# Running half of w1's sums for both chunks early, and pairing the second chunk's attention, in a fused attention and max-out feed-forward kernel

## The chip, the cores and the metric

The kernel runs on one core of a Trainium2 chip. The metric is device time in microseconds (us), lower is better.

The trace records when TensorE's clock is granted at full and when at half rate. The half-rate records are 3.4 us long or a multiple of it, but for the one that the end of the profile can cut: in e12 it begins at 406.85 of 408.3 us, with the work all but done, and makes a mean clock of 0.998. A run's mean clock shows how many others it had: 0.998 to 1.0 for none, about 0.996 for one, 0.992 or less for two or more.

## The reference

```python
def attn(q, k, v, E, F):            # batch 8, heads 8, seq 1024, head_dim 64
    k_proj = einsum('ks,bhsd->bhkd', E, k)       # 64 projected keys
    v_proj = einsum('ks,bhsd->bhkd', F, v)
    scores = q @ k_proj.T / 8
    p = exp(scores - max); p /= p.sum()
    return p @ v_proj
def moe(x, w1, w2, w3, w_out):      # x: 8192 x 512, w1..w3: 512 x 768
    return maximum(maximum(x @ w1, x @ w2), x @ w3) @ w_out
```

The output of the attention, heads side by side, is x. All matrix work is in bf16.

## The kernel before

A batch has four pairs of heads (pair = "g") and two chunks of 512 positions. The four pairs are also the four contraction blocks ("ct") of x @ w, so w's sums over ct 0 and 1 need only pairs 0 and 1. For batch 0, whose inputs are still being loaded, the kernel starts w1 on these two while pairs 2 and 3 are not yet there.

In the traces each engine runs its instructions in the order in which the program gives them. The program has a small clock model of its own; it serves only to choose one of the eight PSUM banks (PSUM is the memory into which TensorE writes) for each result. Several names matter:

- `scores` and `exps`: score matmuls of a pair, and exp of them (pT).
- `z` (sums, then Ln and Exp(-) on ScalarE: zi = 1/sum) and `x` (values, then a VectorE multiplication by zi into xT).
- `k_pair`: projects a pair's keys; VectorE copies them to kpT. `v_pair` does it for values. `kproj(1)`: the keys of batch 1.
- `qp`, `q_duo`: transpose q. `idle(n)`: n filler matmuls on a tile of zeros.

```python
    def up_first(work):                       # batch 0, chunk 0
        ...
        h = six()                             # six banks
        for ct in range(2):
            for jt in jts:
                up_mm(h[jt][0], 0, 0, 0, jt, (ct,), last=1)          # w1
                if ct == 1:
                    copy("sv"[jt % 2], s1[:, jt], *h[jt])            # evict
        then(0)          # q_duo(1), k_pair(2), k_pair(3), scores and exps of
                         # pairs 2 and 3, idle(2), z(2), z(3)
        load_k1()
        h = six()
        for ct in range(2):
            for jt in jts:
                up_mm(h[jt][0], 1, 0, 0, jt, (ct,))                  # w2
            then(1 + ct)                      # 1: v_pair(2); 2: x(2), v_pair(3)
        for jt in jts:
            up_mm(h[jt][0], 1, 0, 0, jt, (2,))
            if jt == 2:
                then(3)                       # x(3)
        ...                                   # w1 ct 2, 3; w2 ct 3; then w3
    def up(b, ch, jt):                        # every other chunk: a step per jt
        ...                                   # w1, w2, w3: four matmuls each
        h1s = ffn_sb.tile([P, CHUNK], FP32, name="h1s")
        nc.scalar.copy(out=h1s, in_=h[0][0])
        ...
        nc.vector.tensor_tensor(out=m12, in0=h[1][0], in1=h1s, op=ALU.max)
        most(hTs[b, ch][:, jt, :], *h[2], m12)                       # VectorE max
    ...
    # plan of batch 0 (chunk, step): second-chunk attention behind w3 and down,
    # then batch 1's attention behind chunk 1's steps
        (0, 6): [za(0, 1, *c1), sc(0, 3, *c1), ld(1)],
        (0, 7): [za(0, 2, *c1)],
        (0, 8): [za(0, 3, *c1)],
        (0, 9): [kproj(1)],
        (1, 0): [kt(1), qp(1, (0,)), qp(1, (1,))],
        ...
        (1, 3): [za(1, 0), sc(1, 3)],
        (1, 4): [za(1, 1)],
        (1, 5): [za(1, 2)],
```

The softmax here doesn't subtract the row's maximum and nothing guards it: scores larger than these inputs give would overflow.

## Time and profile before

| | before |
|---|---|
| time, median | 408.5 us (408.05 to 408.85) |
| span of the profiled run, its mean clock | 407.8 us, 0.996 |
| start of kproj(1) (ends chunk 0 of batch 0) | 48.78 us |
| from there to batch 1's first w1 matmul ("chunk 1's stage") | 29.80 us |

The first part of the page gives busy time per engine, as share of the span. PE is TensorE's matmuls, DVE is VectorE, ACT is ScalarE, POOL is GpSimd.

```profile
span 407.8 us, 6116 instructions
PE 393.8 (97%) x2452; PEld 180.4 (44%) x2497; DVE 202.3 (50%) x311; ACT 192.9 (47%) x281; POOL 34.9 (9%) x46
```

TensorE is nearly always busy, so the gain has to come from its few idle stretches. The table of stretches of the same run shows where they are; a row gives the stretch, its length, and busy time (with the number of instructions) of PE, PEld, DVE, ACT and POOL, then the mean clock, the share of the DMA engines as the view gives it (it can exceed 1) and their GB/s.

```profile
16.50:31.00 14.50, 12.27 (x142) 6.15 (x142) 5.82 (x12) 5.07 (x9) 3.31 (x4) 1.00 1.21 206
...
48.78:78.58 29.80, 29.14 (x239) 13.64 (x243) 17.21 (x26) 17.45 (x23) 2.62 (x3) 1.00 0.83 153
```

Only 2.2 us are idle in the first row. The list of waits for TensorE in 16 to 49 us names what ended each wait; these are the four longest:

```profile
PE banks L288 <- DVE xT L257: 0.8, 1, 0.8
PE banks L207 <- DVE kpT L99: 0.5, 1, 0.5
PE banks L227 <- DVE vp L99: 0.4, 1, 0.4
PE banks L227 <- ACT pT L218: 0.2, 1, 0.2
```

The first is v_pair(3), which waits until x(2)'s multiplication has left the bank; the second is the scores of pair 2, which wait for the kpT copy. No load is in the list.

### The profile page before, as it was taken

The page shows a single profiled execution, that of the slowest core. Times are in us where ns is not written, and L with a number is a line of the kernel's source. Part 1 is how long each engine was busy: PE and PEld are TensorE (multiplying, and loading weights), DVE is VectorE, ACT ScalarE, POOL GpSimd, SP SyncE. Part 2 cuts the span into 40 slices and gives each one's busy share as a digit, 9 for nine tenths or more (in the row PEclk, how much of TensorE's full clock was granted, in tenths as well). Part 3 has the DMA queues.
Part 4 walks back from the last instruction along what each step waited for, and adds up shares of the span by engine and source line. Part 5 has one row for each costly group of instructions (what it writes and reads, how often), then busy time and mean ns, then how long its engine had stood idle before and what let it go on. Part 6 is the DMA issues. An engine that isn't in the chain of part 4 may idle for free.

```text
span 407.8 us, 6116 instructions
## 1 busy us (share of the span) xinstructions
PE 393.8 (97%) x2452; PEld 180.4 (44%) x2497; DVE 202.3 (50%) x311; ACT 192.9 (47%) x281; POOL 34.9 (9%) x46
## 2 busy tenths in 40 slices
PE   7879999999999999999999999999999999999995
PEld 2534454344444544444544445444544444444443
DVE  1429665473465527636453565525464363525251
ACT  2432537623764266547445555537535555432322
POOL 7325002002000200200010002000000000000000
PEclk9899999999999999999999999999999999999999
DMA  9999939959926994893799109960520202020202
GB/s 152 206 207 206 220 98 145 251 122 127 244 42 161 191 247 123 121 242 54 182 184 204 52 13 243 203 161 0 123 87 0 104 2 103 2 103 0 104 0 104
DMA packets 58492, 52.30 MB, mean 128 GB/s; under 512 B 25952, under 2 KB 54112, under 8 KB 58464
## 3 DMA queue, kind: packets, MB, share of 16 engines
q0 software_dynamic: 28496, 28.31, 43.8%
q1 hardware_dynamic: 29824, 23.46, 17.9%
q8 instruction: 19, 0.31, 0.3%
q10 hardware_dynamic: 144, 0.13, 0.1%
q14 instruction: 9, 0.07, 0.1%
HBM read 57.15 MB, written 16.78 MB: 181 GB/s over the span
## 4 chain that ended last, share of the span: by engine, by line
PE 91%; DMA 3%; ACT 2%; DVE 2%; issue 1%; POOL 0%; ACTq 0%; DVEq 0%; POOLq 0%
PE banks L460 60%; PE banks L586 19%; PE banks L227 4%; PE banks L288 4%; DMA k_t<-in_k_dram 2%; PE banks L207 2%; PE banks L299 1%; ACT zl L240 1%; DVE xT L257 1%; ACT pT L218 1%; DMA out_dram<-o_sb 0%; DVE s L99 0%; ACT zi L246 0%; DVE m L551 0%; ACT o_sb L99 0%
## 5 line engine op out<-in xcount | busy, mean ns | idle before, releaser
L460 PE MATMUL banks<-xT,w_sb 128*128 128x512 bf16 x1118 | 255.1, 379 | 2.1 <-issue 0.5
L460 PEld LDWEIGHTS <-w_sb 128*128 128x128 bf16 x1152 | 109.4, 98 | 137.0 <-issue 10.7
L551 DVE TENSOR_TENSOR m<-banks,h1s 128x512 f32<-128x512 f32 x90 | 62.0, 689 | 86.1 <-ACT h1s L547 54.7
L547 ACT COPY h1s<-banks 128x512 f32<-128x512 f32 x90 | 52.5, 583 | 92.5 <-PE banks L460 89.2
L586 PE MATMUL banks<-wout_sb,hT 128*128 128x512 bf16 x369 | 84.8, 379 | 0.7 <-DVE hT L470 0.2
L257 DVE TENSOR_TENSOR xT<-banks,zi 128x1024 bf16<-128x1024 f32 (+1 forms) x36 | 39.8, 1106 | 78.4 <-ACT zi L246 53.7
L470 DVE TENSOR_TENSOR hT<-banks,m 128x512 bf16<-128x512 f32 x90 | 62.3, 692 | 10.1 <-PE banks L227 0.5
L99 ACT COPY o_sb<-banks 128x512 f32<-128x512 f32 (+1 forms) x60 | 34.9, 581 | 53.0 <-PE banks L586 53.0
L586 PEld LDWEIGHTS <-hT 128*128 128x128 bf16 x378 | 36.0, 98 | 45.5 <-issue 3.1
L240 ACT ACTIVATE zl<-banks 128x1024 f32<-128x1024 f32 (+1 forms) x36 | 33.5, 931 | 30.8 <-PE banks L227 30.6
L218 ACT ACTIVATE pT<-banks 128x1024 bf16<-128x1024 f32 (+1 forms) x36 | 33.2, 931 | 9.7 <-PE banks L207 9.7
L246 ACT ACTIVATE zi<-zl 128x1024 f32<-128x1024 f32 (+1 forms) x36 | 34.6, 962 | 1.1
L196 POOL DMA_DIRECT2D q_t<-in_q_dram x7 | 6.2, 883 | 194.1 <-DMA qT<-q_p 72.1
L288 PEld LDWEIGHTS <-efT 128*64 128x64 bf16 x288 | 14.5, 116 | 4.5 <-issue 4.1
L227 PE MATMUL banks<-pT,ones 64*64 64x512 bf16 (+1 forms) x144 | 14.0, 379 | 1.5 <-ACT pT L218 0.9
L207 PE MATMUL banks<-qT,kpT 64*64 64x512 bf16 (+1 forms) x144 | 13.1, 360 | 0.9 <-DVE kpT L99 0.5
L227 PE MATMUL banks<-pT,vp 64*64 64x512 bf16 (+1 forms) x144 | 13.4, 359 | 0.4 <-DVE vp L99 0.4
L99 DVE CAST vp<-banks 64x256 bf16<-64x256 f32 (+1 forms) x18 | 7.1, 397 | 10.7 <-PE banks L288 7.1
L288 PE MATMUL banks<-v_t,efT 128*64 128x256 bf16 (+1 forms) x176 | 10.7, 271 | 0.9 <-DVE xT L257 0.8
L227 PEld LDWEIGHTS <-ones 64*64 64x64 bf16 x144 | 4.5, 103 | 15.4 <-issue 15.3
L99 ACT CAST vp<-banks 64x256 bf16<-64x256 f32 x14 | 5.1, 365 | 7.3 <-PE banks L288 7.1
L99 DVE COPY q_p<-q_t 128x1024 bf16<-128x1024 bf16 x24 | 8.5, 419 | 0.0
(47 smaller groups left out, 106.7 us busy)
## 6 DMA issues: line engine op xcount, KB each, us to landing
out_dram<-o_sb SPq DMA_DIRECT2D x30, 512.0 KB, 3.1
k_t<-in_k_dram POOLq DMA_DIRECT2D x7, 1024.0 KB, 14.0
q_t<-in_q_dram POOLq DMA_DIRECT2D x7, 1024.0 KB, 9.6
v_t<-in_v_dram POOLq DMA_DIRECT2D x7, 1024.0 KB, 18.5
w_sb<-in_moe_w_dram POOLq DMA_DIRECT2D x6, 384.0 KB, 14.8
k_t<-in_k_dram POOLq DMA_DIRECT2D x2, 512.0 KB, 11.0
v_t<-in_v_dram POOLq DMA_DIRECT2D x4, 256.0 KB, 11.5
wout_sb<-in_moe_w_out_dram POOLq DMA_DIRECT2D x1, 768.0 KB, 16.3
```

What stands on the lines that cost most here:

```text
L99: done = {"v": nc.vector.tensor_copy, "s": nc.scalar.copy, "g": nc.gpsimd.tensor_copy}[eng](out=o, in_=i)
L218: nc.scalar.activation(out=pTs[b, g, lo], in_=t, func=AF.Exp, scale=scale)
L227: nc.tensor.matmul(out=t[hp * HALF:(hp + 1) * HALF, c, 0:nsi * HALF], lhsT=w(rows, hp), rhs=p[rows, hp, :], start=True, stop=True,)
L240: nc.scalar.activation(out=zl, in_=t, func=AF.Ln)
L246: nc.scalar.activation(out=zi, in_=zl, func=AF.Exp, scale=-1.0)
L257: nc.vector.tensor_tensor(out=xTs[b][:, g, lo:lo + nsi, :].rearrange("a (c s) p -> a c (s p)", c=2), in0=t, in1=zi, op=ALU.mult,)
L288: nc.tensor.matmul(out=t[hh * HALF:(hh + 1) * HALF, 0:width], lhsT=efT[:, si, kv - 1, :], rhs=qkv[b][kv][:, heads[hh], si, :], start=(si = ...
L460: nc.tensor.matmul(out=h, lhsT=w_sb[i][:, ct, jt * P:(jt + 1) * P], rhs=xTs[b][:, ct, ch * SPC:(ch + 1) * SPC, :], start=(ct == first), st ...
L470: nc.vector.tensor_tensor(out=o, in0=h, in1=other, op=ALU.max)
L547: nc.scalar.copy(out=h1s, in_=h[0][0])
L551: nc.vector.tensor_tensor(out=m12, in0=h[1][0], in1=h1s, op=ALU.max)
L586: nc.tensor.matmul(out=o_ps, lhsT=hTs[b, ch][:, jt, tt * P:(tt + 1) * P], rhs=wout_sb[:, jt, :], start=(jt == 0), stop=(jt == NJT - 1),)
```

## The change

The intent: give TensorE more to do while pairs 2 and 3 are made ready. With the second chunk's attention of pairs 0 and 1 done early, w1's first half can be made for both chunks ahead. The half sums of chunk 1 wait in SBUF (s1[1]) and are added in when chunk 1 comes. The attention of the second chunk is done for two pairs at once, with 128x1024 instead of 128x512 tiles on ScalarE.

```diff
     load_w(0, 0)
+    load_q(LO, slice(SPC, SI))
     load_q(HI, slice(0, SPC))
 ...
+    def za2(b, gs, lo):                       # two pairs: sums, Ln, Exp, values,
+        def f():                              # two multiplications
 ...
+    def add_s1(ch, jt, t, ns):
+        if jt % 2 == 0:
+            nc.vector.tensor_tensor(out=s1[ch][:, jt], in0=t, in1=s1[ch][:, jt], op=ALU.add)
+            return runs("v", clock["pe"], 0.69, ns)
+        h1s = ffn_sb.tile([P, CHUNK], FP32, name="h1s")
+        copy("s", h1s, t, ns)
+        nc.gpsimd.tensor_tensor(out=s1[ch][:, jt], in0=s1[ch][:, jt], in1=h1s, op=ALU.add)
 ...
+        for jt in jts:
+            up_mm(h[jt][0], 0, 0, 0, jt, (0,), last=1)
+        qp(0, (0, 1), *C1)()
+        for jt in jts:
+            up_mm(h[jt][0], 0, 0, 0, jt, (1,), last=1)
+            if jt == 2:
+                sc2(0, (0, 1), SPC, now=True)()
+            copy("sv"[jt in (1, 2, 4, 5)], s1[0][:, jt], *h[jt])
+        q_duo(1)
+        za2(0, (0, 1), SPC)()
+        k_pair(2)
+        k_pair(3)
+        for g in (2, 3):
+            exps(0, g, *C0, scores(0, g, *C0))
         load_k1()
+        for jt in jts:
+            t, ns = bank()
+            up_mm(t, 0, 0, 1, jt, (0, 1), last=1)          # chunk 1
+            if jt in (0, 1):
+                z(2 + jt)
+            copy("sv"[jt in (1, 2, 4, 5)], s1[1][:, jt], t, ns)
+            if jt == 3:
+                v_pair(2)
 ...                                           # x(2), v_pair(3), x(3) among w2's matmuls
     def up(b, ch, jt):
+        split = (b, ch) == (0, 1)
+            if split and i == 0:
+                up_mm(h[i][0], i, b, ch, jt, range(2, NCT - early), first=2)
 ...
+        if split:
+            h1s = s1[1][:, jt]
+            r = add_s1(1, jt, *h[0])
 ...
-                (0, 6): [za(0, 1, *c1), sc(0, 3, *c1), ld(1)],
-                (0, 7): [za(0, 2, *c1)],
-                (0, 8): [za(0, 3, *c1)],
+                (0, 6): [za2(0, (2, 3), SPC), ld(1)],
```

More of the change, by code (lines that the diff above doesn't have):

```diff
@@ L178 @@
     load_w(2, 1)
-    load_q(ALL, slice(SPC, SI))
+    load_q(HI, slice(SPC, SI))
     nc.gpsimd.dma_start(out=wout_sb, in_=moe_w_out.rearrange("(jt p) m -> p jt m", p=P))
@@ L281, in f, with sc2, exps2 @@
             scale_x(b, g, lo, nsi, av)
+        return f
+    N2 = SPC * HALF
+    def sc2(b, gs, lo, now=False):
+        def f():
+            t, ns = two()
+            for i, g in enumerate(gs):
+                for c in range(2):
+                    for hp in range(2):
+                        rows = slice(hp * HALF, (hp + 1) * HALF)
+                        at = g * SI + lo + c * SPC // 2
+                        nc.tensor.matmul(
+                            out=t[c * HALF:(c + 1) * HALF, hp, i * N2:(i + 1) * N2],
+                            lhsT=kpTs[b][rows, g, :],
+                            rhs=qTs[b][rows, at:at + SPC // 2, :],
+                            start=True, stop=True,
+                        )
+            ready = pe(0.4)
+            def exps2():
+                p = att.tile([P, 2, CHUNK], BF16, name="pT", bufs=4)
+                pTs[b, gs, lo] = p
+                nc.scalar.activation(out=p, in_=t, func=AF.Exp, scale=scale)
+                runs("s", ready, 1.0, ns)
+            if now:
+                exps2()
+            else:
+                later.append(exps2)
+        return f
@@ new lines, in za2, with f @@
+    def za2(b, gs, lo):
+        def f():
+            p = pTs[b, gs, lo]
+            z, zns = two()
+            for c in range(2):
+                rows = slice(c * HALF, (c + 1) * HALF)
+                for hp in range(2):
+                    nc.tensor.matmul(
+                        out=z[hp * HALF:(hp + 1) * HALF, c],
+                        lhsT=ones[rows], rhs=p[rows, hp, :], start=True, stop=True,
+                    )
+            ready = pe(0.23)
+            zl = att.tile([P, 2, CHUNK], FP32, name="zl", bufs=1)
+            nc.scalar.activation(out=zl, in_=z, func=AF.Ln)
+            runs("s", ready, 1.0, zns)
+            zi = att.tile([P, 2, CHUNK], FP32, name="zi", bufs=2)
+            nc.scalar.activation(out=zi, in_=zl, func=AF.Exp, scale=-1.0)
+            when = runs("s", ready, 1.0)
+            t, ns = two()
+            for i, g in enumerate(gs):
+                for c in range(2):
+                    rows = slice(c * HALF, (c + 1) * HALF)
+                    for hp in range(2):
+                        nc.tensor.matmul(
+                            out=t[hp * HALF:(hp + 1) * HALF, c, i * N2:(i + 1) * N2],
+                            lhsT=vps[b][rows, 2 * g + hp, :],
+                            rhs=p[rows, hp, i * N2:(i + 1) * N2],
+                            start=True, stop=True,
+                        )
+            pe(0.3)
+            for i, g in enumerate(gs):
+                cols = slice(i * N2, (i + 1) * N2)
+                nc.vector.tensor_tensor(
+                    out=xTs[b][:, g, lo:lo + SPC, :].rearrange("a (c s) p -> a c (s p)", c=2),
+                    in0=t[:, :, cols], in1=zi[:, :, cols], op=ALU.mult,
+                )
+                runs("v", when, 0.69, ns)
@@ L429, in q_duo @@
         )
-    C0 = (0, SPC)
+    C0, C1 = (0, SPC), (SPC, SPC)
     idle(11)
@@ L471, in most, with up_first @@
         return runs("v", max(clock["pe"], ready), 0.69, ns)
-    def up_first(work):
-        def then(key):
-            run_later()
-            for f in work.get(key, []):
-                f()
-        s1 = ffn_sb.tile([P, NJT, CHUNK], FP32, name="s1", bufs=1)
-        s2 = ffn_sb.tile([P, NJT, CHUNK], FP32, name="s2", bufs=1)
+    s1 = [ffn_sb.tile([P, NJT, CHUNK], FP32, name=f"s1_{ch}", bufs=1) for ch in range(2)]
+    def add_s1(ch, jt, t, ns):
[5 more added lines that the diff above has]
+        nc.gpsimd.tensor_tensor(out=s1[ch][:, jt], in0=s1[ch][:, jt], in1=h1s, op=ALU.add)
+        return clock["s"] + 1.3
+    def up_first():
         hTs[0, 0] = ffn_sb.tile([P, NJT, CHUNK], BF16, name="hT")
@@ L489, in up_first @@
         h = six()
-        for ct in range(2):
-            for jt in jts:
-                up_mm(h[jt][0], 0, 0, 0, jt, (ct,), last=1)
-                if ct == 1:
-                    copy("sv"[jt % 2], s1[:, jt], *h[jt])
-        then(0)
-        load_k1()
-        h = six()
-        for ct in range(2):
-            for jt in jts:
-                up_mm(h[jt][0], 1, 0, 0, jt, (ct,))
-            then(1 + ct)
+        for jt in jts:
[12 more added lines that the diff above has]
+            exps(0, g, *C0, scores(0, g, *C0))
+        load_k1()
+        for jt in jts:
[6 more added lines that the diff above has]
+                v_pair(2)
+        h = six()
+        for jt in jts:
+            up_mm(h[jt][0], 1, 0, 0, jt, (0,))
+            if jt == 1:
+                x(2)
+            if jt == 3:
+                v_pair(3)
+        for jt in jts:
+            up_mm(h[jt][0], 1, 0, 0, jt, (1,))
+            if jt == 1:
+                x(3)
         for jt in jts:
             up_mm(h[jt][0], 1, 0, 0, jt, (2,))
-            if jt == 2:
-                then(3)
+        joined = [0.0] * NJT
         for jt in jts:
@@ L508, in up_first @@
             up_mm(t, 0, 0, 0, jt, (2, 3), first=2)
-            if jt % 2:
-                copy("s", s2[:, jt], t, ns)
-                nc.gpsimd.tensor_tensor(
-                    out=s1[:, jt], in0=s1[:, jt], in1=s2[:, jt], op=ALU.add
-                )
-                added = clock["s"] + 1.3
-            else:
-                nc.vector.tensor_tensor(out=s1[:, jt], in0=t, in1=s1[:, jt], op=ALU.add)
-                added = runs("v", clock["pe"], 0.69, ns)
-            up_mm(h[jt][0], 1, 0, 0, jt, (3,))
-            if jt % 2 == 0:
-                most(s1[:, jt], *h[jt], s1[:, jt], added)
-            elif jt > 2:
-                most(s1[:, jt - 2], *h[jt - 2], s1[:, jt - 2], last)
-            if jt % 2:
-                last = added
-        most(s1[:, 5], *h[5], s1[:, 5], last)
-        then(4)
+            joined[jt] = add_s1(0, jt, t, ns)
+            up_mm(h[jt][0], 1, 0, 0, jt, (3,))
+            for j in ((jt,) if jt % 2 == 0 else (jt - 2,) if jt > 2 else ()):
+                most(s1[0][:, j], *h[j], s1[0][:, j], joined[j])
+        most(s1[0][:, 5], *h[5], s1[0][:, 5], joined[5])
         for jt in jts:
@@ L529, in up_first @@
             up_mm(t, 2, 0, 0, jt, range(NCT))
-            most(hTs[0, 0][:, jt, :], t, ns, s1[:, jt])
-            then(5 + jt)
+            most(hTs[0, 0][:, jt, :], t, ns, s1[0][:, jt])
+            if jt == 2:
+                qp(0, (2, 3), *C1)()
+            if jt == 4:
+                sc2(0, (2, 3), SPC, now=True)()
     def up(b, ch, jt):
@@ L537, in up @@
         early = jt == 0
+        split = (b, ch) == (0, 1)
         for i in range(3):
             h.append(bank())
-            up_mm(h[i][0], i, b, ch, jt, range(NCT - early))
+            if split and i == 0:
+                up_mm(h[i][0], i, b, ch, jt, range(2, NCT - early), first=2)
+            else:
+                up_mm(h[i][0], i, b, ch, jt, range(NCT - early))
             done.append(clock["pe"])
@@ L545, in up @@
                 done[i] = clock["pe"]
-        h1s = ffn_sb.tile([P, CHUNK], FP32, name="h1s")
-        nc.scalar.copy(out=h1s, in_=h[0][0])
-        r = runs("s", done[0], 0.6, h[0][1])
+        if split:
+            h1s = s1[1][:, jt]
+            r = add_s1(1, jt, *h[0])
+        else:
+            h1s = ffn_sb.tile([P, CHUNK], FP32, name="h1s")
+            nc.scalar.copy(out=h1s, in_=h[0][0])
+            r = runs("s", done[0], 0.6, h[0][1])
         run_later()
@@ L609, in plan @@
         if b == 0:
-            c1 = (SPC, SPC)
             return {
-                (0, 6): [za(0, 1, *c1), sc(0, 3, *c1), ld(1)],
-                (0, 7): [za(0, 2, *c1)],
-                (0, 8): [za(0, 3, *c1)],
+                (0, 6): [za2(0, (2, 3), SPC), ld(1)],
                 (0, 9): [kproj(1)],
@@ L672 @@
             if (b, ch) == (0, 0):
-                c1 = (SPC, SPC)
-                def attend():
-                    q_duo(1)
-                    k_pair(2)
-                    k_pair(3)
-                    for g in (2, 3):
-                        exps(0, g, *C0, scores(0, g, *C0))
-                    idle(2)
-                    for g in (2, 3):
-                        z(g)
-                up_first({
-                    0: [attend],
-                    1: [lambda: v_pair(2)],
-                    2: [lambda: x(2), lambda: v_pair(3)],
-                    3: [lambda: x(3)],
-                    5: [qp(0, (0, 1), *c1)],
-                    6: [qp(0, (2, 3), *c1)],
-                    7: [sc(0, 0, *c1)],
-                    8: [sc(0, 1, *c1)],
-                    10: [za(0, 0, *c1), sc(0, 2, *c1)],
-                })
-                run_later()
+                up_first()
                 behind(0, NJT - 1)
```

## The prediction

> **What bounds it now.** TensorE: 97% busy over a span of 407.8 us (page, part 1), 91% of the chain that ended last. From 50 us on it is over 98% busy at full clock, and the change removes no matmul there. Only the first 50 us can give something. The table of stretches shows 12.27 us of TensorE busy in 16.5-31 us: 2.2 us idle, plus 0.4 us of filler matmuls (idle(2)). The waits there: kpT (0.5), pT (0.2), twice the bank that scale_x holds (0.8 and 0.3), and small ones. These 2.6 us (0.6%) are all that the change can win. Loads are not the limit: in 16-50 us no TensorE wait names a DMA. By the load queue's bytes, k's high half lands about 18.7 us; 0.25 MB more ahead of it adds 1.3 us, still in time.
>
> **What changes, by durations of the trace.**
> - Removed: idle(2), 0.4 us. Exp/Ln/Exp of 128x512 tiles (0.60 us) are paired to 128x1024 (1.03).
> - Moved: 12 w1 matmuls of chunk 1 (12 x 0.216 = 2.6 us) ahead of w2, as filler for pairs 2 and 3; the second chunk's attention of pairs 0, 1 (about 1.9 us of TensorE) to around the second w1 quarter.
> - Added: six evictions of half sums (0.6 us each); in chunk 1 three VectorE adds (0.69) and three GpSimd adds (1.31).
>
> **Critical path.** The moved matmuls stand *after* the scores of pairs 2 and 3 in program order, and so do not fill a new wait. VectorE's order is now: q copy, two multiplications of za2, then kpT of pairs 2 and 3. The Trainium skill, "TensorE: Matmul & The Clock Gate", Part 1, says VectorE is strict FIFO (this case's trace shows program order). So kpT waits for zi of za2. My estimate from the durations: second-chunk scores end about 19.65, exp 20.65, sums 21.3, Ln 22.3, Exp 23.3, two multiplications 24.5, kpT 24.75. TensorE ends k_pair(3) about 22.35: about 2.4 us idle before L207's scores. Around x(2) and v_pair(3), which share one free pair of banks, some 0.7 us of waits stay. Sum: -2.6 + 2.4 + 0.7 = +0.5 us.
> In chunk 1 (50-79 us) the chain sums-Ln-Exp-multiply (64.9 to 68.5 us now) already held TensorE for 0.35 us; with 2.6 us less matmul there and a GpSimd add before VectorE's maximum in odd steps, +0.3 us.
> The same section of the skill gives a free-running activity window of 3.4 us after which an idle TensorE drops to half clock. The trace has such a record: half clock for 3.4 us from about 13.7 us, after thin work. The new gap may earn another, at about 1.2 us; half a chance: +0.6. I halve the total of +1.4, as the wait may be overestimated.
>
> **Prediction: 409.2 us**, 8 in 10 between 406.3 and 411.6. Faster by over 2%: 0.02; within 2%: 0.95; slower by over 2%: 0.03.
>
> **What would show it.** Right: a TensorE wait of 1.5-3 us at the scores, released by the kpT copy, near 22-25 us; VectorE waiting for zi just before the paired multiplications; the old waits of 0.8 and 0.5 us gone or smaller; chunk 1's steps of batch 0 shorter by about 0.4 us each, with more bank waits. A half-clock record near 24 us would show the clock step.
> Wrong: no such wait at the scores, or under 1 us of idle in 16-35 us; then the time is about 406.5. If chunk 1 stalls by more than 1 us on GpSimd adds, or batch 1's q, loaded later, delays its transposes, it is above 411.

## More of the kernel before

Times of a kernel are medians over several executions. The span in a profile is about 1.8 us shorter than the time of the same run.

## The result, and the profile after

The change is slower: 413.91 us median (412.80 to 414.14, 4 runs) against 408.57 us (4 runs). The ratio is 1.0127, with a 95% interval of 1.0106 to 1.0148. Ratios here are the mean time of one kernel's fast runs over that of the kernel before in the same rounds, so they are not quite the ratio of the medians quoted. In class this is "within 2%", but the time lies above the predicted range.

The page of the changed kernel:

```profile
span 412.3 us, 6145 instructions
PE 397.8 (96%) x2487; PEld 179.9 (44%) x2487; DVE 207.4 (50%) x319; ACT 190.9 (46%) x273; POOL 39.6 (10%) x50
```

TensorE's waits in 16 to 50 us:

```profile
PE banks L208 <- DVE kpT L99: 2.8, 1, 2.8
PE banks L208 <- ACT pT L219: 0.7, 1, 0.7
PE banks L228 <- DVE vp L99: 0.4, 1, 0.4
PE banks L359 <- DVE xT L258: 0.3, 1, 0.3
```

The wait for kpT grew from 0.5 to 2.8 us. The timelines show why. First TensorE, start and length of each group in us, with the idle time before it and its releaser in brackets:

```profile
21.05 0.41 PE L323 MATMUL banks<-pT,ones 64*64 64x512 bf16 x4
21.29 0.51 PE L339 MATMUL banks<-pT,vp 64*64 64x256 bf16 x8
21.73 0.69 PE L477 MATMUL banks<-efT,k_t 128*64 128x64 bf16 x32
25.19 0.30 PE L208 MATMUL banks<-qT,kpT 64*64 64x256 bf16 x4 [2.76 <-DVE kpT L99]
26.19 0.30 PE L208 MATMUL banks<-qT,kpT 64*64 64x256 bf16 x4 [0.70 <-ACT pT L219]
26.42 1.03 PE L531 MATMUL banks<-xT,w_sb 128*128 128x512 bf16 x2
```

Then VectorE in the same run, over the same stretch:

```profile
21.64 0.68 DVE L99 COPY qT<-banks 128x1024 bf16<-128x1024 bf16 x1
23.71 1.29 DVE L348 TENSOR_TENSOR xT<-banks,zi 128x512 bf16<-128x512 f32 x2 [1.39 <-ACT zi L332]
24.92 0.35 DVE L99 CAST kpT<-banks 128x64 bf16<-128x64 f32 x2
```

k_pair(3) leaves TensorE about 22.4 us, but the kpT copies stand in VectorE's queue behind two multiplications, and these wait for zi of the early attention. So the scores of pairs 2 and 3, and everything behind them in TensorE's order, wait too. In "26.42 1.03 ... x2" two matmuls take 1.03 us, where a matmul at full clock takes 0.216 us behind another: TensorE has just dropped to half clock. The rows of stretches, where the mean clock is the third figure from the end, show it:

```profile
25.00:26.00 1.00, 0.30 (x4) 0.22 (x5) 0.26 (x3) 0.46 (x1) 0.28 (x1) 1.00 1.17 216
26.00:27.00 1.00, 0.81 (x6) 0.24 (x5) 0.00 (x0) 0.60 (x2) 0.00 (x0) 0.73 1.16 204
27.00:28.00 1.00, 1.00 (x7) 0.27 (x6) 0.00 (x0) 0.22 (x2) 0.00 (x0) 0.50 1.17 210
28.00:29.00 1.00, 1.00 (x6) 0.13 (x4) 0.18 (x1) 0.97 (x2) 0.00 (x0) 0.50 1.14 206
```

Chunk 1's stage, and TensorE's waits of 50 to 90 us in the same run:

```profile
53.81:83.02 29.21, 26.94 (x231) 12.41 (x231) 19.16 (x29) 15.99 (x20) 6.48 (x6) 1.00 0.96 173
```

```profile
PE banks L531 <- DVE m L646: 0.8, 1, 0.8
PE banks L228 <- DVE xT L258: 0.7, 1, 0.7
PE banks L681 <- DVE hT L541: 0.5, 1, 0.5
PE banks L531 <- DVE hT L541: 0.3, 1, 0.3
```

The stage has twelve matmuls less, 12 x 0.216 = 2.6 us, but is only 0.6 us shorter: TensorE now idles 2.3 us in it, where it idled 0.7.

The sum between the two profiled runs, by stretch: w1 begins at 16.45 and 16.56 us. From there to kproj(1), before takes 32.33 us and after 37.25 us. After has 2.6 us of matmul more in it, so 2.3 us are lost. In chunk 1's stage 2.0 us are lost (29.21 + 2.6 - 29.80). From batch 1 to the end the two agree within 0.1 us. That makes the 4.5 us between the spans. The 5.3 us between the medians are more, most likely because the profiled run of before had a half-clock record at about 12.5 to 15.9 us; of the 44 runs of before that were taken beside the experiments below, 35 had a mean clock of 0.998 or more. Of the four runs of the changed kernel, three had 0.992 and one 0.996, and the latter's span is 1.3 us shorter (411.0 against about 412.3). So one half-clock record costs about 1.3 us here; in e1 below the spans of runs with none, one and two records (408.1, 409.3 to 409.6 and 410.7 us) are as far apart.

### The profile page after: what moved, and what is told of

It is laid out like the page before. It is cut to its first block, busy times and chain, and to the rows that moved or that the text cites. A ratio compares the mean times of both kernels' runs of the same rounds, so it can differ in the third digit from the quotient of the medians.

```text
span 412.3 us, 6145 instructions
## 1 busy us (share of the span) xinstructions
PE 397.8 (96%) x2487; PEld 179.9 (44%) x2487; DVE 207.4 (50%) x319; ACT 190.9 (46%) x273; POOL 39.6 (10%) x50
## 4 chain that ended last, share of the span: by engine, by line
PE 92%; DMA 3%; DVE 2%; ACT 1%; issue 1%; POOL 1%; DVEq 0%; ACTq 0%; POOLq 0%
PE banks L531 61%; PE banks L681 19%; PE banks L228 4%; PE banks L359 4%; DMA k_t<-in_k_dram 2%; PE banks L208 2%; PE banks L370 1%; DVE m L646 1%; ACT pT L219 1%; DMA out_dram<-o_sb 0%; DVE hT L541 0%; DVE xT L348 0%; POOL s L553 0%; DVE s L99 0%; ACT zi L332 0%
## 5 line engine op out<-in xcount | busy, mean ns | idle before, releaser
L531 PE MATMUL banks<-xT,w_sb 128*128 128x512 bf16 x1152 | 259.5, 381 | 1.1 <-DVE m L646 0.8
L646 DVE TENSOR_TENSOR m<-banks,h1s 128x512 f32<-128x512 f32 x84 | 57.9, 689 | 81.9 <-ACT h1s L642 52.3
L258 DVE TENSOR_TENSOR xT<-banks,zi 128x1024 bf16<-128x1024 f32 (+1 forms) x32 | 37.0, 1157 | 72.6 <-ACT zi L247 53.0
L241 ACT ACTIVATE zl<-banks 128x1024 f32<-128x1024 f32 (+1 forms) x32 | 31.1, 971 | 29.0 <-PE banks L228 28.6
L219 ACT ACTIVATE pT<-banks 128x1024 bf16<-128x1024 f32 (+1 forms) x32 | 30.9, 973 | 8.3 <-PE banks L208 8.3
L247 ACT ACTIVATE zi<-zl 128x1024 f32<-128x1024 f32 (+1 forms) x32 | 32.1, 1003 | 1.0
L208 PE MATMUL banks<-qT,kpT 64*64 64x512 bf16 (+1 forms) x128 | 12.1, 369 | 3.9 <-DVE kpT L99 2.8
L228 PE MATMUL banks<-pT,ones 64*64 64x512 bf16 (+1 forms) x128 | 13.1, 398 | 0.4 <-ACT pT L219 0.3
L228 PE MATMUL banks<-pT,vp 64*64 64x512 bf16 (+1 forms) x128 | 12.3, 370 | 1.1 <-DVE xT L258 0.7
L553 POOL TENSOR_TENSOR s<-s,h1s 128x512 f32<-128x512 f32 x6 | 7.6, 1271 | 33.2 <-ACT h1s L99 33.1
## 6 DMA issues: line engine op xcount, KB each, us to landing
w_sb<-in_moe_w_dram POOLq DMA_DIRECT2D x6, 384.0 KB, 13.7
```

The lines of the kernel that those rows point to most:

```text
L219: nc.scalar.activation(out=pTs[b, g, lo], in_=t, func=AF.Exp, scale=scale)
L228: nc.tensor.matmul(out=t[hp * HALF:(hp + 1) * HALF, c, 0:nsi * HALF], lhsT=w(rows, hp), rhs=p[rows, hp, :], start=True, stop=True,)
L241: nc.scalar.activation(out=zl, in_=t, func=AF.Ln)
L247: nc.scalar.activation(out=zi, in_=zl, func=AF.Exp, scale=-1.0)
L258: nc.vector.tensor_tensor(out=xTs[b][:, g, lo:lo + nsi, :].rearrange("a (c s) p -> a c (s p)", c=2), in0=t, in1=zi, op=ALU.mult,)
L531: nc.tensor.matmul(out=h, lhsT=w_sb[i][:, ct, jt * P:(jt + 1) * P], rhs=xTs[b][:, ct, ch * SPC:(ch + 1) * SPC, :], start=(ct == first), st ...
```

## The experiments

Theory A has three parts. The order of kpT on VectorE holds TensorE. The gap that this makes costs a half-clock record too. The split of w1 takes its 2.6 us in the front, and chunk 1 gives back little, as other engines hold it. The rivals are stated with the runs. The table gives all of them; "stage" is chunk 1's stage in the profiled run.

| run | median us | ratio to before (95%) | mean clock of runs | stage us |
|---|---|---|---|---|
| before | 408.26 to 408.84 | 1 | mostly 0.998 to 1.0 | 29.80 |
| the change | 413.91 | 1.0127 (1.0106 to 1.0148) | 0.992 to 0.996 | 29.21 |
| e1 kpT first | 411.20 | 1.0070 (1.0053 to 1.0088) | 0.992 to 1.0 | 29.22 |
| e2 no early w1 | 411.02 | 1.0069 (1.0052 to 1.0086) | 0.987 to 0.992 | 29.80 |
| e3 adds on VectorE | 414.45 | 1.0150 (1.0137 to 1.0164) | 0.992 | 29.17 |
| e4 gap filled | 411.75 | 1.0074 (1.0059 to 1.0089) | 0.998 to 1.0 | 29.23 |
| e5 three blocks of six | 411.45 | 1.0086 (1.0070 to 1.0102) | 0.990 to 0.991 | 28.89 |
| e6 e1 and e2 | 409.26 | 1.0034 (1.0012 to 1.0055) | 0.986 to 0.996 | 29.80 |
| e7 before, spaced | 408.49 | 1.0007 (0.9994 to 1.0020) | 0.998 to 1.0 | 29.81 |
| e8 before, new front | 409.17 | 1.0022 (1.0006 to 1.0038) | 0.995 to 1.0 | 29.81 |
| e9 e6, other banks, filler | 407.44 | 0.9972 (0.9951 to 0.9994) | 0.999 to 1.0 | 29.80 |
| e10 e9, zi later | 411.55 | 1.0067 (1.0042 to 1.0092) | 0.989 to 0.996 | 29.80 |
| e11 e4 without early w1 | 409.87 | 1.0031 (1.0003 to 1.0059) | 0.992 to 0.999 | 29.80 |
| e12 e9 with early w1 | 409.43 | 1.0012 (0.9985 to 1.0039) | 0.998 to 1.0 | 29.21 |

All runs gave a correct result.

### e1: kpT ahead of the multiplications

```diff
-        za2(0, (0, 1), SPC)()
+        za2(0, (0, 1), SPC, hold=True)()   # all but its two multiplications
         k_pair(2)
         k_pair(3)
+        held.pop()()                       # the two multiplications
```

> The changed kernel with one edit of order on VectorE: the two multiplications of the first paired attention stand behind the two kpT copies, banks unchanged. Theory A (the program order on VectorE makes kpT wait for zi, which holds TensorE 2.8 us): the 2.8 us wait at the scores goes below 0.5 us; but the scores of pair 3 still wait for the exponential of pair 2, which now stands behind zi on ScalarE, and w1's chunk-1 sums wait for xT; so of the 3.5 us of both waits some 1.7 us come back, and the half-clock record may go (another 1.2 us): 1.7 to 2.9 us faster than the changed kernel, 411 to 412.2 us. Rival B (kpT is not the limit, the waiting is elsewhere, in evictions or loads): less than 0.5 us gained.

Measured: 411.20 us, 2.7 us faster, as theory A has it. At an equal clock it is 1.6 us (spans of 410.7 against 412.3 us at 0.992, 409.4 against 411.0 at 0.996), and some of its runs had fewer half-clock records. TensorE's timeline in e1:

```profile
22.30 0.30 PE L208 MATMUL banks<-qT,kpT 64*64 64x256 bf16 x4 [0.22 <-ACT zl L331]
23.87 0.30 PE L208 MATMUL banks<-qT,kpT 64*64 64x256 bf16 x4 [1.27 <-ACT pT L219]
```

The 2.76 us before the first scores are down to 0.22. The wait before the second scores is longer: both pairs' scores use the same PSUM banks, and pair 2's exponential, which frees them, now stands behind zi on ScalarE. That choice of banks was also behind the 0.70 us in the changed kernel; the prediction had not seen it.

### e2: no early w1

```diff
-        for jt in jts:
-            t, ns = bank()
-            up_mm(t, 0, 0, 1, jt, (0, 1), last=1)
-            ...
+        z(2)
+        z(3)
+        v_pair(2)
...
-        split = (b, ch) == (0, 1)
+        split = False
```

> The changed kernel without the early half of w1 for chunk 1 (no early matmuls, evictions or adds; chunk 1 as in the kernel before); the early paired attention stays. Theory A (splitting w1 costs about 2 us in chunk 1, as 2.6 us of matmul leave a stage that is held by ScalarE, VectorE and GpSimd, while as a filler it returns about 1 us ahead of chunk 0's w2): about 1 us faster than the changed kernel, 412.2 to 413.4 us, with chunk 1's stage (kproj(1) to batch 1's first w1) about 29.8 us instead of 29.2, though with 12 matmuls more; the wait at the scores stays at 2.8 us. Rival B (the early matmuls are worth their 2.6 us as filler, all loss is in the early attention): 414.5 us or more.

Measured: 411.02 us, 2.9 us faster, where I expected about 1. The direction and the stage (29.80 us) are those of theory A; rival B is excluded. Why the size was off is not shown: perhaps the early matmuls gave even less back as filler than I had allowed, and the half-clock records that stayed had less matmul to slow. The wait at the scores, which I expected to stay at 2.8 us, was 2.4. To take the clock out as far as possible, e11 repeats this with the gap filled.

### e3: the adds of chunk 1 on VectorE

```diff
+        if ch == 1:
+            nc.vector.tensor_tensor(out=s1[ch][:, jt], in0=t, in1=s1[ch][:, jt], op=ALU.add)
+            return ...
         h1s = ffn_sb.tile([P, CHUNK], FP32, name="h1s")
```

> The changed kernel, but all six adds of chunk 1's half sums on VectorE (0.69 us each, straight from PSUM) in place of three ScalarE copies and three GpSimd adds; banks unchanged. Theory A (the chain of copy, GpSimd queue with the loads' issues ahead of it, 1.3 us add, maximum holds banks and the last hT): the waits of 0.8 us (maximum of step 3) and 0.5 us (hT of step 5) shrink, 0.8 to 1.5 us faster than the changed kernel, 412.4 to 413.1 us. Rival B (VectorE's load in chunk 1 is the limit): same or slower, 413.8 us or more.

Measured: 414.45 us, stage 29.17 us against 29.21. My theory of the GpSimd chain fell, as far as a gain goes. The wait of 0.8 us for the maximum is gone, but others came in its place. VectorE's timeline in e3, from batch 1's first pair to the third:

```profile
70.67 1.23 DVE L258 TENSOR_TENSOR xT<-banks,zi 128x1024 bf16<-128x1024 f32 x1 [1.13 <-ACT zi L247]
71.82 0.68 DVE L549 TENSOR_TENSOR s<-banks,s 128x512 f32<-128x512 f32 x1
72.60 0.69 DVE L650 TENSOR_TENSOR m<-banks,s 128x512 f32<-128x512 f32 x1
73.40 0.69 DVE L541 TENSOR_TENSOR hT<-banks,m 128x512 bf16<-128x512 f32 x1
74.27 1.23 DVE L258 TENSOR_TENSOR xT<-banks,zi 128x1024 bf16<-128x1024 f32 x1 [0.18 <-ACT zi L247]
75.41 0.68 DVE L552 TENSOR_TENSOR s<-banks,s 128x512 f32<-128x512 f32 x1
76.20 0.69 DVE L650 TENSOR_TENSOR m<-banks,s 128x512 f32<-128x512 f32 x1
77.00 0.69 DVE L541 TENSOR_TENSOR hT<-banks,m 128x512 bf16<-128x512 f32 x1
77.60 1.22 DVE L258 TENSOR_TENSOR xT<-banks,zi 128x1024 bf16<-128x1024 f32 x1
```

A step takes VectorE 3.6 us (70.67 to 74.27): four instructions one behind the other, of which the last three need each other's results. TensorE's work in such a step is ten matmuls and the pair's sums and values, about 2.8 us. From 70.67 to 78.82 us VectorE is busy for 7.54 of 8.15 us. My reading is that with the add on VectorE it is VectorE that paces these steps, and that with the adds on GpSimd the result comes as late by another way. That is argued, not shown: the multiplications still waited 1.13 and 0.18 us for zi, and the chain of sums, Ln, Exp and multiplication is a rival that no run takes away. What is shown is that moving the add does not help.

### e4: filler in the gap

```diff
         k_pair(3)
+        for _ in range(11):
+            nc.tensor.matmul(out=psum_t[:, 7, :], lhsT=warm[:, 0:P], rhs=warm, start=True, stop=True)
         for g in (2, 3):
```

> The changed kernel with eleven filler matmuls (2.4 us) between k_pair(3) and the scores, in the gap where TensorE waits for kpT; they delay nothing. Theory A (the gap with thin work before it costs a window at half clock): the half-clock record near 27 us is gone, and with it about 1.2 us: 412.5 to 412.9 us, while the wait at the scores shrinks to 0.3 us by the filler. Rival B (the record has another cause or costs nothing): 413.7 us or more.

Measured: 411.75 us, 2.2 us faster with nothing but filler added; no run had as much half-clock time as one record of 3.4 us (clocks 0.998 to 1.0; one record makes 0.996). Theory A holds, and the effect is larger than the 1.2 us expected. e3, whose front is that of the changed kernel, had two such records in a row in its profile (mean clock 0.992 in all its runs) and none in the early work. The profile of the changed kernel had one early (12.8 to 16.2 us) and one behind the gap (26.5 to 29.9). The filler comes too late to remove an early record, so part of the 2.2 us against the changed kernel may be chance.

The rows below are 3.4 us of the changed kernel just before its clock drops, and two such stretches of e4, over the filler and behind it:

```profile
23.05:26.46 3.41, 0.57 (x9) 0.37 (x10) 1.55 (x4) 1.23 (x2) 1.54 (x2) 1.00 1.18 211
20.00:23.40 3.40, 3.14 (x46) 1.67 (x47) 1.97 (x5) 1.75 (x2) 1.58 (x2) 1.00 1.22 205
23.40:26.80 3.40, 2.70 (x24) 0.99 (x24) 0.75 (x2) 2.47 (x5) 0.88 (x1) 1.00 1.16 209
```

The kept traces say more than "the gap" does. In each of the 14 profiles the clock changes only at whole multiples of 3.41 us from its first change, and this grid lies elsewhere in each run. Up to 400 us the clock drops 13 times, each time after a window of the grid in which TensorE was busy for 0.6 to 2.0 us; every window at full clock that no drop follows was busy for 2.1 us or more. (In the last 10 us two windows of 1.5 and 1.9 us bring none, and a few matmul records can be missing from a trace, so the line is not sharp.) So what counts here is the busy share of such a window, not one long gap: e1 has no wait above 1.3 us there and still drops, after a window with 1.77 us. Where the grid falls decides whether the early work drops too, and whether the gap costs one record or two.

### e5: three of the six blocks

```diff
-            t, ns = bank()
-            up_mm(t, 0, 0, 1, jt, (0, 1), last=1)
+            if jt < 3:
+                t, ns = bank()
+                up_mm(t, 0, 0, 1, jt, (0, 1), last=1)
...
-        split = (b, ch) == (0, 1)
+        split = (b, ch) == (0, 1) and jt < 3
```

> The changed kernel with the early half of w1 for chunk 1 made for column blocks 0 to 2 alone instead of all six. Theory A (what chunk 1 does not give back is lost in its steps 3 to 5, where an attention pair per step loads ScalarE and VectorE, and one add more makes VectorE the limit): steps 0 to 2 give their 1.3 us back nearly whole, so chunk 1's stage takes 28.5 to 28.8 us (29.2 with all six, 29.8 with none) and the time falls by about 2 us against the changed kernel, to 411.5 to 412.3 us. Rival B (each early block costs the same): chunk 1's stage about 29.5 us, and the time half way between the changed kernel and the run without early w1, about 412.4 us or more.

Measured: 411.45 us, stage 28.89 us. The time is where theory A put it, but does not decide: by ratio, half way between the changed kernel and e2 is 1.0098, inside e5's interval. The stage does: it is 0.1 us above A's range and well below B's 29.5. Blocks 0 to 2 give 0.9 of their 1.3 us back. Blocks 3 to 5, which meet batch 1's attention, give back less than nothing: the stage with all six is 0.3 us longer than with three.

### e6: both repairs

The edits of e1 and e2 together.

> Both repairs on the changed kernel: the two kpT copies ahead of the paired multiplications, and no early w1. If the two losses are separate, it is about 1.6 us faster than the run without early w1 alone (more where the half-clock windows go): 408.8 to 409.8 us; the remainder against the kernel before is then the wait of pair 3's scores for the exponential behind zi. If the early w1 was needed as filler once kpT is in time, it gains less than 0.5 us: 410.5 us or more.

Measured: 409.26 us. The losses are separate. What remains against the kernel before is mostly clock, and not, or not alone, the wait of pair 3's scores (0.8 us) that I expected: at 0.995 to 0.996 its spans are 406.6 to 406.8 us, and those of before at that clock 407.4 and more. But all six of its runs had such records, against nine of the 44 of before.

### e7 and e8: ideas of the change on the kernel before

e7 sets x(2) and v_pair(3) apart among w2's matmuls, as the change does. e8 also moves q_duo(1), k_pair(2) and k_pair(3) between w1's two quarters and the scores among the second, and takes idle(2) away.

```diff
                 up_mm(h[jt][0], 1, 0, 0, jt, (ct,))
+                if ct == 1 and jt == 1:
+                    x(2)
+                if ct == 1 and jt == 5:
+                    v_pair(3)
```

> The kernel before with one idea of the change alone: x(2) and v_pair(3) stand apart between w2's matmuls (after its second, and after its sixth of the second quarter) instead of one behind the other. Theory (of the change's intent, that the waits of 0.8 us for the bank and 0.3 us are worth closing): both go, 0.7 to 1.1 us faster than the kernel before. Rival (the time is given back at once, as later work waits for loads or VectorE): less than 0.3 us.

> As the run before (spaced), and q, k and the scores of pairs 2 and 3 moved between and among the two quarters of w1 of chunk 0 in place of after them, with no second-chunk work ahead: the interleaving of the change without its new dependence on zi. The filler of 0.4 us and the waits of 0.5 and 0.2 us go: 1.5 to 2.1 us faster than the kernel before, if loads are in time (q's second half is then needed about 33.5 us, just as it lands; its transposes stand one step later for that). If a load wait of over 0.5 us takes its place, under 1.2 us.

Measured: 408.49 us (same as before) and 409.17 us (0.2% slower). Both expectations of a gain fell, and e7's trace says why. TensorE's timeline in e7, a run at full clock; up to x(2) it executes the kernel before unchanged:

```profile
17.08 0.64 PE L299 MATMUL banks<-ident,q_t 128*64 128x128 bf16 x16
18.85 0.69 PE L406 MATMUL banks<-efT,k_t 128*64 128x64 bf16 x32 [1.14 <-DMA k_t<-in_k_dram]
...
26.92 5.92 PE L460 MATMUL banks<-xT,w_sb 128*128 128x512 bf16 x25
33.54 0.64 PE L299 MATMUL banks<-ident,q_t 128*64 128x128 bf16 x16 [0.70 <-DMA q_t<-in_q_dram]
```

At full clock TensorE gets to k's second half before it has landed and waits 1.14 us, and what the spacing wins is waited for at q's second half. In the profiled run of before, the early half-clock record had delayed TensorE by so much that no load was late from 16 us on. So in most runs the front of the kernel before is probably paced by loads, and the idle time that the change set out to fill was not all there to be won; no profile of the kernel before itself at full clock was taken. e8, which asks for k's second half earlier, waits 1.19 us for it although its profile has the early half-clock record.

### e9 and e10: a repaired front

```diff
+        exps(0, 2, *C0, scores(0, 2, *C0))
+        idle(3)
+        exps(0, 3, *C0, scores(0, 3, *C0))
+        held.pop()()                       # the two multiplications
+        idle(2)
```

This is e6 with these lines in place of the loop over the scores; the bank model is told of the late multiplications, and then gives the two scores different banks. e10 also puts Ln and Exp of the early attention behind the exponentials of pairs 2 and 3.

> The changed kernel without early w1, with the kpT copies ahead of the paired multiplications, the scores of pairs 2 and 3 in different banks, and five filler matmuls in the two waits that stay (three between the scores, two before the sums), to hold the clock. If the rest of the loss was the half-clock windows, they go and it equals the kernel before or is slightly faster: 406.8 to 408.3 us. If a loss is in the early attention itself, it stays at 409 us or more.

> As the run before, but the whole of Ln, Exp and multiplication of the early paired attention stands behind the exponentials of pairs 2 and 3 on ScalarE too. If the exponentials of pairs 2 and 3 behind zi are what is left, this is up to 0.5 us faster than that run; if the sums of pairs 2 and 3 now wait for ScalarE instead, it is 0.5 to 1.5 us slower.

Measured: e9 takes 407.44 us, ratio 0.9972 (0.9951 to 0.9994), so it is slightly faster than the kernel before, in class "same". All its runs were at full clock. The early attention does win a little where TensorE would wait for k: the wait of 1.14 us in e7 is 0.17 us in e9's timeline.

```profile
19.66 0.69 PE L486 MATMUL banks<-efT,k_t 128*64 128x64 bf16 x32 [0.17 <-DMA k_t<-in_k_dram]
```

e10 is 4.1 us slower than e9, more than the 0.5 to 1.5 us expected of the bad case: it has waits for Ln of 1.1, 0.7 and 0.6 us, and half-clock records came back (0.989 to 0.996). In its profile one record, from 29.2 us, follows these waits (TensorE busy for 1.47 us of the window before). The other, from 8.8 us, lies ahead of everything that the edit moves, so not all of the 4.1 us are owed to it.

### e11 and e12: the early w1 at full clock

e11 is e4 with the edit of e2; e12 is e9 with the early w1 put back.

> The changed kernel with the gap filled (as in e4_fill_gap) and without early w1: the same comparison as between the changed kernel and e2_no_w1_ahead, but now both at full clock. Theory A (splitting w1 takes its 2.6 us in the front and gives 0.6 us of it back in chunk 1, whatever the clock): about 2 us faster than e4_fill_gap, 409.4 to 410.2 us. Rival B (most of that loss was half-clock windows that fell on the early matmuls): less than 1 us faster, 410.8 us or more.

> The repaired front of e9_full_clock with the early w1 for chunk 1 put back: the change's full intent without its wait for kpT. Theory A (the early w1 only moves 2.6 us into the front and chunk 1 gives 0.6 us back): about 2 us slower than e9_full_clock, 409.0 to 410.2 us, chunk 1's stage 29.2 us. Rival B (with kpT in time the early w1 is good filler): within 0.7 us of e9_full_clock, 408.1 us or less.

Measured: e11 409.87 us against e4's 411.75; some runs of e11 have half-clock records, and those at 0.999 have spans of 406.9 to 407.4 us against e4's 408.8 to 410.0 at 0.998 to 1.0. e12 409.43 us against e9's 407.44. The early w1 costs about 2 us with the wait for kpT and without it, and at full clock. The stages are again 29.80 and 29.21 us. The two pairs were compared across calls and chips, so the difference by ratio (0.4%, 1.6 to 1.8 us) is as good a figure. One more thing shows in e12's profile, its slowest run (span 408.3 us, e9's 405.1): at 16.79 us the transposes for the second chunk's attention of pairs 0 and 1 wait 1.12 us for q, the very load that the change put ahead. About 1.1 us of the 3.2 us between these two profiles is that wait; the other 2.1 us fit the split.

## Why the prediction was wrong

The direction of the argument (no gain, for a new wait at the scores) was right, and the class. The time, 413.9 us, lies 2.3 us above the range. Step by step:

- **The wait at the scores** (predicted about 2.4 us, released by kpT): 2.76 us, and e1 shows the order on VectorE to be its cause. Right. The Trainium skill, "TensorE: Matmul & The Clock Gate", Part 1, states that VectorE's queue is strict FIFO, and the trace agrees: the kpT copies ran at 24.92 us, right behind the multiplications, though their data were there at about 22.4.
- **The sum of the front, +0.5 us**: 2.3 us in the profiled runs, of which one half-clock record is 1.3, so about 1.0. (Of the old waits counted there, the second of xT, 0.3 us, was not in the front: it stands at 68.53 us.) The extra part is near the 0.70 us of pair 3's scores, which wait for a bank that pair 2's exponential holds. I had looked at banks for x(2) and v_pair(3) but not for the scores.
- **"In chunk 1 ... +0.3 us"**: this is the step that failed, the term that was mis-sized most. It measured 2.0 us (stage 29.21 us, with 2.6 us less matmul than the 29.80). The prediction had chunk 1's steps shorter by about 0.4 us each, which is nearly all of the 2.6 us; the whole stage became 0.6 us shorter. The prediction did name the case in its last lines (a stall of over 1 us in chunk 1, then above 411 us), with the GpSimd adds as cause. e2, e11 and e12 show that it goes with the split, e5 that it belongs to steps 3 to 5, where an attention pair per step runs. I had seen that a chain held TensorE there already, for 0.35 us, and should have concluded that matmuls taken from a stage with so little slack are not given back. Which of the other engines holds it in the changed kernel itself is not settled: there a GpSimd add (75.41 us, 1.27 us) is in the chain that ended last, but e3 takes GpSimd out without a gain and finds VectorE with little slack, and no run relieves VectorE or ScalarE alone.
- **The half-clock record, "half a chance: +0.6"**: the second large miss. e4 shows that the record behind the scores comes of the idle time there, and it came in every profile that kept this gap unfilled (the changed kernel, e2, e3, e5). Filling the gap gained 2.2 us. I had placed the record of before at 13.7 us; it was about 12.5 to 15.9. I also took the profiled run of before, at 0.996, for a typical one, where most of its runs had no such record.
- **"I halve the total of +1.4"**: halving for doubt went the wrong way. The terms I was unsure of could only be larger.
- **"Loads are not the limit"**: true of the profiled run, probably wrong for most runs: e7 at full clock waits 1.14 and 0.70 us for loads, and e12 1.12 us for the q that was put ahead ("still in time"). It did not cause the error of the time, but it means that even the 2.6 us of possible gain was too high.

The parts add up roughly: about 1.0 us of order and banks in the front, 2.0 us in chunk 1, and some 2.2 us of clock make 5.2 of the 5.3 us. That they fit so closely is partly luck. The first comes from profiles with an early half-clock record; between the full-clock profiles of e4 and e7, kproj(1) starts 3.0 us later, and 2.6 of these are the moved matmuls.

## What to carry to other kernels

Work moved ahead as filler is worth its time only if it stands, in program order, before the wait that it should fill, and if the stage that it leaves was held by the engine that it relieves. Before putting a long chain (sums, Ln, Exp, multiply) ahead of a short copy on an in-order engine, ask who waits for that copy. And look at the clock of several runs before taking one profile for the usual case: a slow stretch early in a run can hide a load limit, and a gap of under 3 us, or several short ones close together, can cost a second time by the clock.

## What the Trainium skill lacked or had wrong

- "TensorE: Matmul & The Clock Gate", section "HAM oscillation", gives as the abstract rule that idle gaps over about 3.4 us are to be avoided. Here an idle gap of 2.76 us was enough, with thin work around it (TensorE busy 0.57 of the 3.4 us ahead of the drop). The early record of before came after a window in which TensorE was busy for 1.5 of 3.4 us, and over all profiles the line lay between 2.0 and 2.1 us of busy time (see e4). The record's length (3413 and 3414 ns in the traces) agrees with the page's window.
- The same page, Part 1, says that the window runs free and the effect varies from run to run, and the runs agree. It lacks that the variation also changes what limits a kernel: one profile of before, at 0.996, shows no load wait from 16 us on, while e7 at 1.0 executes the same start in the same order and waits 1.14 us for a load.
- The pages that I used do not say that a few filler matmuls inside an unavoidable wait can pay for themselves in the middle of a kernel: with eleven of them e4 was 2.2 us faster than the changed kernel.
